# Lightning attention and a leaky-ReLU MLP on one core: k and q block loads on SyncE's queue, three chunks at a time

## The chip, the cores and the metric

The kernel runs on one core of one Trainium2 chip. Times are device microseconds of that core; the metric is the median over several runs of the whole kernel.

## What is computed

Inputs are `q`, `k`, `v` (4 batches, 8 heads, 768 positions, head size 64), a decay `lam` per head, and weights `w_in` (512 x 2048) and `w_out` (2048 x 512), which arrive as 64-bit floats and are turned into 32-bit ones on the chip. The reference, cut to what matters:

```
for b in range(nb):                       # blocks of 64 positions
    intra = einsum('bhic,bhjc->bhij', qb, kb) * Dmask      # lam ** (i - j), i >= j
    intra = einsum('bhij,bhjd->bhid', intra, vb)
    inter = einsum('bhid,bhde->bhie', qb * lam_pow, kv_state)
    out[:, :, sl] = intra + inter
    kv_state = lam_block * kv_state + einsum('bhsd,bhse->bhde', kb * rev_pow, vb)
x = out.transpose(0, 2, 1, 3).reshape(3072, 512)
h = x @ w_in
return maximum(0.01 * h, h) @ w_out
```

## The kernel before

The 3072 rows of x are 24 chunks of 128 tokens, six groups of four chunks. Every value in the MLP is split into three parts (h, l, m), so that each product is made of three products on TensorE.

Stages. First, attention of the first chunks and the conversion of `w_in` (to about 96 us in the profile). Then "rounds", one per chunk, mixed with "up" products, which are x times `w_in` for one group and one of eight slices of 256 columns of d_ff. Last, the "down" products with `w_out` (L658, from 354 us). An up product for a whole group (L599) has six blocks of four matmuls of 512 columns on the PSUM banks b10, b11 and b2; ACT rescales a bank (L617), then applies leaky ReLU into one of two `gs` buffers (L620), and SP stores `gs` to `G` in DRAM (L623). The down stage reads `G` back (L633).

A round (`round_of`, L487) has the own block's product into `po` (L291), then the next chunk's scores and state update into `psc` (L291), then the second half of the inter-block product into `po`. Before that second half, TensorE waits for `seen_po`, a copy of two columns of `po` by DVE or ACT (L448). Then ACT and DVE make xh, xl and xm of the chunk (L464, L465, L467). DVE multiplies the scores by the decay (L409), POOL scales k and q (L379, L383).

How k and q come in. The products need k and q with head dimension on partitions (`kTs`, `qTs`, two buffers each, by chunk parity). Up to chunk 11 TensorE transposes them (L363). From chunk 12 (`DV`) `load_subs` (L325) loads blocks of 32 x 32 elements so that a DVE transpose of 32 x 32 squares (`turn`, L340, its instruction L343) finishes the work: 16 loads of 32 KB for k and 16 for q, each for two chunks. k goes by SP's queue into `raw[2]`, q by ACT's queue, first into `raw[1]`, then into q's former buffer in `att`. k in its natural form and v are loaded as well (L316, L348), on SP.

`w_out` in the meantime: `w_out` (L573) loads each slice's two halves (512 KB each, L526, SP's queue) into `raw[0]` or `raw[1]`; ACT makes three pieces (L535, L537, L539), DVE joins them (L541, L542) into `w32`, and SP stores that to DRAM (L576). `w_out_parts` (L578) reads it back (L580) into buffers that lie over attention's `att` memory, once attention is over, and makes h, l and m of it (L548, L550, L553, L559), in the place of `w_in`'s parts.

What sets the order. A program-time planner (`Plan`, L37 on) records each operation with an engine, an estimated duration, its dependencies and a rank (the place in the list `seq`, L696, plus an offset), and `emit` (L81) lays them out engine by engine: at each step the operation that can start first, then the lowest rank. A result counts as there after the duration and a lag; for a DMA the lag is 3.5 us:

```
LAG = {"PE": 0.25, "ACT": 0.1, "DVE": 0.1, "POOL": 0.12, "DMA": 3.5}
ends[u].append((free[e], e))
```

"DMA" stands for SP's queue. Each engine and each queue then runs its list strictly in this order. `seen_po` may go to DVE or ACT, as the planner finds. In `seq`, the first 41 entries are written by hand (they reach round 11); then come 32 up products of the groups 2 to 5, with the rounds from 12 to 23 after every second one, and one `w_out` slice after every third.

Of the kernel before, what the change touches and what calls it, by code (L numbers as in the profile page):

```python
# [36 lines left out]
class Plan:  # L37
# [7 lines left out]
    def __init__(self):  # L45
        self.ops, self.last, self.rank = [], {}, 0.0
        self.chain, self.chains = None, {}
        self.warm = 0.0
        self.first = {"PE": 0.0, "ACT": 0.0, "DVE": 3.4, "POOL": 0.0, "DMA": 0.2}
        self.cold, self.idle, self.spare = 6.0, None, None  # L50
# [10 lines left out]
    def add(self, eng, us, fn, reads=(), writes=(), rank=0.0):  # L61

        n, deps = len(self.ops), set()
        for k in reads:
            w, r = self.last.setdefault(k, [None, []])
            if w is not None:
                deps.add(w)
            r.append(n)
        for k in writes:
            w, r = self.last.setdefault(k, [None, []])  # L70
            if w is not None:
                deps.add(w)
            deps.update(r)
            self.last[k] = [n, []]
        deps.discard(n)
        ways = {eng: us} if isinstance(eng, str) else dict(zip(eng, us))
        if self.chain is not None:
            self.chains[self.chain].append(n)
        self.ops.append((ways, fn, deps, (self.rank + rank, n), set(writes)))

    def emit(self):  # L81
# [30 lines left out]
        while len(done) < n:  # L112
# [23 lines left out]
            for u in users[i]:  # L136
                ends[u].append((free[e], e))
                left[u] -= 1
                if not left[u]:
                    for x in self.ops[u][0]:  # L140
                        able[x].add(u)
# [19 lines left out]
def kernel(  # L161
# [28 lines left out]
    NRAW = 3  # L190
    SUBQ, SUBR, SUBD = ("DMA", "ACT"), 5.0, 0.0

    DV = 12
    C4 = P // 4
    HALF = (slice(0, D), slice(D, 2 * D))
    assert DV % 2 == NCB % 2 == 0 and D == 64 and KO == HP == 4 and SEQ % C == 0 and NCH % GC == 0 and d_model == T == 512 and NP % 4 == 0

# [21 lines left out]
    lows = [sb([P, d_model], f"low{i}", I32) for i in range(2)]  # L219
    w32 = sb([P, 2, d_model], "w32")  # L220
    tt = [raw[-1][:, i * T:(i + 1) * T] for i in range(2)]
    gs = [sb([P, 2, T], f"gs{i}") for i in range(2)]
# [3 lines left out]

    NA = 8608
    att = sb([P, NA], "att")
# [8 lines left out]
    ident = part(P)  # L237
    kqv_f = [part(2 * H * D) for _ in range(3)]
    kqv = [[x[:, i * H * D:(i + 1) * H * D].rearrange("p (h d) -> p h d", h=H) for i in range(2)] for x in kqv_f]
# [23 lines left out]
    plan.idle, plan.spare, plan.warm = busy, "b10", 1.3 + 0.22 * WARM  # L263
    add = plan.add

    def factors_k():
# [42 lines left out]
    def load_kq(c):  # L309
        b, n, i = of(c)  # L310
        for src, x, nm in ((k, 0, "k"), (q, 1, "q")):
            y, dst = src[b, :, n * C:(n + 1) * C, :], kqv[x][i]

            def go(y=y, dst=dst):
                for z in range(2):
                    nc.sync.dma_start(out=dst[:, z * HP:(z + 1) * HP, :], in_=y[z::2].rearrange("h p d -> p h d"))  # L316
            if nm == "k" or c < DV:
                add("DMA", 1.15 if c < DV else 1.5, go, [], [f"{nm}{i}"])

    def subs(c):  # L320

        two = ((k, raw[-1], [f"raw{NRAW - 1}"]), (q, raw[-2], [f"raw{NRAW - 2}"]) if c < DV + 2 else (q, kqv_f[1], ["q0", "q1"]))
        return [(x, y.rearrange("p (y t) -> p y t", y=HP), keys) for x, y, keys in two]

    def load_subs(c):  # L325
        b, n, i = of(c)
        for nm, eng, (src, sub, keys) in zip("kq", SUBQ, subs(c)):
            add("DVE", 0.0, lambda: None, [], keys)
            for y in range(HP):
                for a in range(4):  # L330
                    h = y // 2 + (2 * y + a // 2) % HP * 2
                    z = src[b, h, n * C:(n + 2) * C, a % 2 * C4:(a % 2 + 1) * C4]
                    o = sub[a * C4:(a + 1) * C4, y, :]
                    add(eng, 0.58 if eng == "DMA" else 0.45,
                        lambda o=o, z=z, e=nc.sync if eng == "DMA" else nc.scalar: e.dma_start(  # L335
                            out=o.rearrange("j (m i) -> j m i", i=C4), in_=z.rearrange("(m j) i -> j m i", j=C4)),
                        keys, [f"{nm}s{y}{a}"], rank=SUBR + SUBD * (4 * y + a))
            add("DMA", 0.0, lambda: None, [f"{nm}s{y}{a}" for y in range(HP) for a in range(4)], [f"{nm}s"])

    def turn(c):  # L340
        i = c % 2
        for nm, (_, sub, keys), dst in zip("kq", subs(c - i), (kTs[i], qTs[i])):
            add("DVE", 0.7, lambda a=dst, b=sub: nc.vector.transpose(out=a, in_=b[:, :, i * C:(i + 1) * C]),  # L343
                keys + [f"{nm}s"] + [f"{nm}s{y}{a}" for y in range(HP) for a in range(4)], [f"{nm}T{i}"])

    def load_v(c):
        b, n, i = of(c)
        add("DMA", 1.15, lambda: nc.sync.dma_start(out=kqv[2][i], in_=v[b, :, n * C:(n + 1) * C, :].rearrange("h p d -> p h d")),  # L348
            [], [f"v{i}"])
# [137 lines left out]
    def round_of(c):  # L487
# [14 lines left out]
        if DV <= c + 3 < NCH:  # L502
            turn(c + 3)
        if DV <= c + 4 < NCH and c % 2 == 0:
            load_subs(c + 4)
# [7 lines left out]
    def to_float32(kind, p, h, dst, key, after=()):  # L513

        nonlocal n_raw
        j, n_raw = n_raw % (len(raw) - (kind == "wo")), n_raw + 1
        r, low, kl = raw[j], lows[n_raw % 2], f"low{n_raw % 2}"
        d = dst.bitcast(I32)

        def load():  # L520
            r64 = r.bitcast(I64)
# [11 lines left out]

        add("DMA", 1.6, load, after, [f"raw{j}"])
        add("ACT", 0.67, lambda: nc.scalar.activation(out=dst, in_=words(1, F32), func=AF.Abs, scale=2.0 ** -110),  # L535
# [25 lines left out]

    w32f = w32.rearrange("p h n -> p (h n)")

    def w_in(p):
# [7 lines left out]

    def w_out(p, after):  # L573
        for h in range(2):
            to_float32("wo", p, h, w32[:, h, :], f"w32{h}", after)
        add("DMA", 1.5, lambda: nc.sync.dma_start(out=WO[p], in_=w32f), ["w320", "w321"], [f"WO{p}"])  # L576

# [9 lines left out]
    def up(g, p, lo=0, hi=GC):  # L587
# [20 lines left out]
        for fs in blocks:  # L608
# [9 lines left out]
            for i, f in enumerate(fs):  # L618
                add("PE", us, lambda f=f, d=b[:, i, :]: product(d, f, 2), keys("m"), [kb])
            add("ACT", ns, lambda b=b, r=r: nc.scalar.activation(out=r, in_=b, func=AF.Prelu, bias=0.0, scale=1.0 / WS, alpha=0.01),  # L620
                [kb], [f"gs{jg}"], rank=-1.5)
        add("DMA", 1.5 * (hi - lo) / GC + 0.1,
            lambda: nc.sync.dma_start(out=G[g][p].rearrange("p (f t) -> p f t", f=2)[:, :, toks], in_=y), [f"gs{jg}"], [f"G{g}{p}"])  # L623

# [21 lines left out]
    def down(g, p):  # L646

        nonlocal n_t
        for tb in range(GC):
# [51 lines left out]
           ("up", 1, 4)]  # L701
    nxt, n_out = 3 * GC, 0
    steps = [(g, p) for g in range(2, NG) for p in range(NP)]
    for n, (g, p) in enumerate(steps):
# [4 lines left out]
        if nxt < NCH and nxt // GC < g + 2 and n % 2 == 0:  # L709
            seq.append(("r", nxt))  # L710
            nxt += 1
        if n_out < NP and n % 3 == 1:
            seq.append(("wo", n_out, ["G%d%d" % steps[n - 1]]))
            n_out += 1
# [7 lines left out]
    for n, x in enumerate(seq):  # L722
        plan.rank = float(n)
        if x[0] in "abr":
            {"a": alone, "b": begun, "r": round_of}[x[0]](x[1])
# [48 lines left out]
```

## Time and profile before

| | |
|---|---|
| runs | 621.29, 622.35, 626.31 us |
| median | 622.35 us |
| profiled execution's own time | 623.09 us |
| its span | 621.3 us |
| granted TensorE clock, mean | 0.996 |

Transfers that the change touches (from the profile's list of DMA issues; the last column is the median time from issue to landing):

| transfer | queue, line | count | size | us to landing |
|---|---|---|---|---|
| k blocks into `raw` | SP, L335 | 96 | 32 KB | 2.5 |
| q blocks into `att` | ACT, L335 | 80 | 32 KB | 3.0 |
| q blocks into `raw` | ACT, L335 | 16 | 32 KB | 2.6 |
| `w_out` halves | SP, L526 | 16 | 512 KB | 5.9 |
| stores of `gs` to `G` (whole groups) | SP, L623 | 45 | 512 KB | 3.4 |
| v | SP, L348 | 24 | 256 KB | 4.3 |

How to read the profile: PE is TensorE's matmuls and PEld its weight loads, DVE is VectorE, ACT ScalarE, POOL GpSimd; SPq and ACTq are DMA issues on the queues of SyncE and ScalarE. A timeline row has start, length, engine, line, operation, output<-input, size and count; in brackets the idle time just before it and what ended it. Busy TensorE time has modelled ends, so gaps are best read from start to start. The medians above are of one execution.

### The profile page before, as it was taken

Reading aid. Unit: us, or ns where it says so; the run is one execution under the profiler, and the core shown is the slowest. Engines: PE = TensorE matmul, PEld = TensorE weight load, DVE = VectorE, ACT = ScalarE, POOL = GpSimd, SP = SyncE. Lnnn points to the kernel's source line nnn. Section 1 sums busy time; section 2 is a strip of 40 time slices with the busy share of each in tenths; the row PEclk is TensorE's granted clock in tenths of the full one; section 3 lists DMA queues with packets and bytes.
Section 4 is the critical chain, followed back from the end, with each engine's and each line's share of the span. In section 5 each row is a group of like instructions: output and inputs, shape, how many; then the busy total and the mean of one; then the engine's idle time right before and its main releaser. Section 6 shows DMA issues by size and latency. Waiting matters only on the chain.

```text
span 621.3 us, 13134 instructions
## 1 busy us (share of the span) xinstructions
PE 606.5 (98%) x5482; PEld 504.4 (81%) x5482; DVE 306.9 (49%) x401; ACT 266.8 (43%) x426; POOL 90.9 (15%) x95
## 2 busy tenths in 40 slices
PE   8799999999999998999999999999999999999997
PEld 7588987898888877888778888888888888888885
DVE  4679883610354335434255863735545454535531
ACT  3598884334456455556564622312222312214111
POOL 4752422410223123221000000000000000000000
PEclk9899999999999999999999999999999999999999
DMA  9888867572788878885765752433424333433201
GB/s 202 222 254 266 230 190 165 137 160 104 207 203 233 248 202 231 208 252 187 258 232 212 245 192 69 164 108 101 170 71 142 127 111 126 135 103 120 84 1 68
DMA packets 143259, 104.68 MB, mean 168 GB/s; under 512 B 118112, under 2 KB 120160, under 8 KB 143200
## 3 DMA queue, kind: packets, MB, share of 16 engines
q1 hardware_dynamic: 112592, 92.30, 48.9%
q10 hardware_dynamic: 30608, 11.55, 7.6%
q8 instruction: 43, 0.70, 0.5%
q14 instruction: 16, 0.13, 0.1%
HBM read 68.16 MB, written 35.65 MB: 167 GB/s over the span
## 4 chain that ended last, share of the span: by engine, by line
PE 87%; DMA 8%; ACT 2%; DVE 1%; SPq 1%; issue 1%; POOL 0%; DVEq 0%; ACTq 0%
PE b L599 37%; PE b L658 18%; PE po L658 11%; PE psc L658 11%; DMA att<-in_q_dram 4%; PE pt L658 3%; PE po L291 3%; PE psc L291 3%; DMA att<-in_v_dram 2%; DMA att<-in_k_dram 1%; DMA raw<-in_moe_w_out_dram 1%; PE pt L363 1%; SPq L335 1%; ACT low L537 1%; PE b L258 1%
## 5 line engine op out<-in xcount | busy, mean ns | idle before, releaser
L640 ACT ACTIVATE xh<-att 128x1024 fp32r<-128x1024 f32 x48 | 50.9, 1061 | 147.3 <-PE po L658 145.9
L641 DVE SCALAR_TENSOR_TENSOR xl<-att,xh 128x1024 fp32r<-128x1024 f32 x48 | 58.7, 1223 | 99.4 <-ACT xh L640 99.3
L599 PE MATMUL b<-xh,wh 128*128 128x512 f32 (+3 forms) x416 | 105.8, 377 | 0.0
L599 PE MATMUL b<-xm,wm 128*128 128x512 f32 (+3 forms) x416 | 104.6, 382 | 0.8 <-ACT b L617 0.8
L599 PE MATMUL b<-xl,wl 128*128 128x512 f32 (+3 forms) x416 | 105.2, 376 | 0.0
L599 PEld LDWEIGHTS b<-xl,wl 128*128 128x128 f32 x416 | 75.5, 188 | 14.5
L599 PEld LDWEIGHTS b<-xh,wh 128*128 128x128 f32 x416 | 75.0, 188 | 14.2
L599 PEld LDWEIGHTS b<-xm,wm 128*128 128x128 f32 x416 | 73.3, 188 | 16.2 <-ACT b L617 2.3
L620 ACT ACTIVATE gs<-b 128x512 f32<-128x512 f32 (+2 forms) x98 | 57.7, 589 | 54.7 <-PE b L599 46.9
L617 ACT ACTIVATE b<-b 128x512 f32<-128x512 f32 (+2 forms) x98 | 55.8, 576 | 59.1 <-PE b L599 47.2
L658 PE MATMUL b<-wh,xh 128*128 128x512 f32 x192 | 74.7, 389 | 0.0
L658 PE MATMUL b<-wl,xl 128*128 128x512 f32 x192 | 74.7, 389 | 0.0
L643 DVE SCALAR_TENSOR_TENSOR xm<-xl,xh 128x1024 fp32r<-128x1024 f32 x48 | 58.8, 1226 | 4.8
L383 POOL TENSOR_TENSOR att<-att 128x512 f32<-128x512 f32 (+1 forms) x24 | 30.3, 1263 | 83.9 <-PE po L291 31.1
L658 PEld LDWEIGHTS b<-wh,xh 128*128 128x128 f32 x192 | 36.0, 187 | 7.6
L658 PEld LDWEIGHTS b<-wl,xl 128*128 128x128 f32 x192 | 36.1, 188 | 7.4
L419 POOL TENSOR_TENSOR att<-att 128x256 f32<-128x256 f32 x40 | 33.7, 843 | 38.5 <-DVE att L416 35.0
L409 DVE TENSOR_TENSOR att<-psc,att 128x512 f32<-128x512 f32 x24 | 16.5, 688 | 43.4 <-PE psc L291 43.4
L658 PE MATMUL po<-wm,xm 128*128 128x512 f32 (+1 forms) x100 | 37.2, 381 | 0.7 <-ACT raw L680 0.7
L658 PE MATMUL pt<-wm,xm 128*128 128x512 f32 x96 | 37.3, 389 | 0.0
L658 PE MATMUL b<-wm,xm 128*128 128x512 f32 x96 | 37.3, 389 | 0.0
L658 PE MATMUL psc<-wh,xh 128*128 128x512 f32 x96 | 37.3, 389 | 0.0
(69 smaller groups left out, 785.3 us busy)
## 6 DMA issues: line engine op xcount, KB each, us to landing
att<-g SPq DMA_DIRECT2D x48, 512.0 KB, 3.3
g<-gs SPq DMA_DIRECT2D x45, 512.0 KB, 3.4
raw<-in_moe_w_in_dram ACTq DMA_DIRECT2D x16, 512.0 KB, 5.0
raw<-in_moe_w_out_dram SPq DMA_DIRECT2D x16, 512.0 KB, 5.9
att<-in_k_dram SPq DMA_DIRECT2D x48, 128.0 KB, 4.0
att<-in_v_dram SPq DMA_DIRECT2D x24, 256.0 KB, 4.3
out_dram<-gs SPq DMA_DIRECT2D x23, 256.0 KB, 2.0
wo<-w SPq DMA_DIRECT2D x8, 512.0 KB, 3.2
```

Of the source, the lines that this page charges most:

```text
L258: nc.tensor.transpose(out=b1[0][:, 0:P], in_=ident, identity=ident)
L291: nc.tensor.matmul(dst[HALF[cols]], lhsT=lhsT[HALF[rows]], rhs=rhs[HALF[rows]], start=start, stop=True, skip_group_check=True)
L383: add(eng, us, lambda: e.tensor_tensor(o, x, _bc(pow_q, 2, 2)[:, :, m, :], op=ALU.mult), ["fq", dep], [f"qsT{i}"])
L409: add("DVE", 0.69, lambda: nc.vector.tensor_tensor(sc, psc[:, :, lower, :], decay, op=ALU.mult), ["psc", "fk"], ["sc"])
L419: add("POOL", 0.7, lambda new=new, j=j: nc.gpsimd.tensor_tensor(state[(j + 1) % 4], new, _bc(lam_c, 2, D), op=ALU.mult), [f"st{j % 4}", "f ...
L599: nc.tensor.matmul(dst, lhsT=w[z][:, kk * 2 * P + f * P:kk * 2 * P + (f + 1) * P], rhs=x[z][:, kk, toks], start=start and kk == 0, stop=kk ...
L617: add("ACT", ns, lambda b=b: nc.scalar.activation(out=b, in_=b, func=AF.Copy, bias=0.0, scale=S + 1.0), [], [kb], rank=-1.5)
L620: add("ACT", ns, lambda b=b, r=r: nc.scalar.activation(out=r, in_=b, func=AF.Prelu, bias=0.0, scale=1.0 / WS, alpha=0.01), [kb], [f"gs{jg} ...
L640: add("ACT", 1.05, lambda: nc.scalar.activation(out=h, in_=graw[j], func=AF.Copy, bias=0.0, scale=NEAR), reads, wr("h"))
L641: add("DVE", 1.25, lambda: nc.vector.scalar_tensor_tensor(l, graw[j], 1.0, h.bitcast(F32), op0=ALU.mult, op1=ALU.subtract), reads + [f"rh{ ...
L643: add("DVE", 1.25, lambda: nc.vector.scalar_tensor_tensor(m, l.bitcast(F32), -S, h.bitcast(F32), op0=ALU.mult, op1=ALU.add), [f"rh{j}", f" ...
L658: nc.tensor.matmul(acc[tb][z // 2][:, cols], lhsT=ring[j][z][:, f * T + tb * P:f * T + (tb + 1) * P], rhs=W[pp][z][:, f * d_model:(f + 1) ...
```

## The change

Block loads: both k and q go by SP's queue, 48 KB each, for three chunks instead of two. k lies in two pieces in `raw[1]` and `raw[2]`; q of chunks 12 to 14 in three pieces in `w32` and the two `lows`, later in q's former buffer, made longer by 512 elements per partition. One DVE transpose per piece. `w_out` keeps `raw[0]` alone, and its halves are entries of `seq` of their own, one after each up product until all 16 are placed.

Planner: loads and stores made by `move` in the later part (`steady`: rounds, up products and `w_out` entries after the hand-written list) count with 0.5 us of queue time (1.0 for k's pair, 0.75 for a block load) instead of a transfer's duration, with 4 us (2 us for stores of `gs`) added before a result counts as there, and with a rank offset of -8. Block loads have rank offsets of their own: from 4.0 up by 0.2 for each of the 16 places (earlier part) or 0.4 (later part). The first two blocks (chunks 12 to 17) are made in the earlier part, with 0.55 us each; the other two in the later part.

The core of the diff:

```diff
-        self.warm = 0.0
+        self.warm, self.slack, self.more = 0.0, 0.0, {}
...
+        if self.slack:
+            self.more[n] = self.slack
...
-                ends[u].append((free[e], e))
+                ends[u].append((free[e] + self.more.get(i, 0.0), e))
...
-    SUBQ, SUBR, SUBD = ("DMA", "ACT"), 5.0, 0.0
+    TURN = 3
+    SLACK, GSLACK = 4.0, 2.0
+    SUBL, FIRST = 0.75, -8.0
...
-    NA = 8608
+    NA = 9120
...
-    kqv_f = [part(2 * H * D) for _ in range(3)]
+    kqv_f = [part(2 * H * D + (TURN - 2) * HP * C * (i == 1)) for i in range(3)]
...
+    steady = False
+
+    def length(us, issue=0.5):
+
+        return issue if steady else us
+
+    def move(us, fn, reads, writes, issue=0.5, rank=0.0, slack=SLACK):
+
+        plan.slack = slack if steady else 0.0
+        if steady and not rank:
+            rank = FIRST
+        add("DMA", length(us, issue), fn, reads, writes, rank=rank)
+        plan.slack = 0.0
...
-                add("DMA", 1.15 if c < DV else 1.5, go, [], [f"{nm}{i}"])
+                move(1.15, go, [], [f"{nm}{i}"], issue=1.0)
 
     def subs(c):
 
-        two = ((k, raw[-1], [f"raw{NRAW - 1}"]), (q, raw[-2], [f"raw{NRAW - 2}"]) if c < DV + 2 else (q, kqv_f[1], ["q0", "q1"]))
-        return [(x, y.rearrange("p (y t) -> p y t", y=HP), keys) for x, y, keys in two]
+
+        n = TURN * C
+        def rows(x, lo, hi):
+            return x[:, :(hi - lo) * n].rearrange("p (y t) -> p y t", t=n), lo, hi
+        ks = [(*rows(raw[-2], 0, 2), [f"raw{NRAW - 2}"]), (*rows(raw[-1], 2, 4), [f"raw{NRAW - 1}"])]
+        if c < DV + TURN:
+            return ks, [(*rows(w32f, 0, 2), ["w320", "w321"])] + [
+                (*rows(lows[i].bitcast(F32), 2 + i, 3 + i), [f"low{i}"]) for i in range(2)]
+        return ks, [(*rows(kqv_f[1], 0, HP), ["q0", "q1"])]
 
     def load_subs(c):
         b, n, i = of(c)
-        for nm, eng, (src, sub, keys) in zip("kq", SUBQ, subs(c)):
-            add("DVE", 0.0, lambda: None, [], keys)
...
-                    add(eng, 0.58 if eng == "DMA" else 0.45,
-                        lambda o=o, z=z, e=nc.sync if eng == "DMA" else nc.scalar: e.dma_start(
-                            out=o.rearrange("j (m i) -> j m i", i=C4), in_=z.rearrange("(m j) i -> j m i", j=C4)),
-                        keys, [f"{nm}s{y}{a}"], rank=SUBR + SUBD * (4 * y + a))
...
+        for nm, src, pieces in zip("kq", (k, q), subs(c)):
+            for sub, lo, hi, keys in pieces:
+                add("DVE", 0.0, lambda: None, [], keys)
...
+                        move(0.55, lambda o=o, z=z: nc.sync.dma_start(
+                                out=o.rearrange("j (m i) -> j m i", i=C4), in_=z.rearrange("(m j) i -> j m i", j=C4)),
+                            keys, [f"{nm}s{y}{a}"], issue=SUBL, rank=4.0 + (0.4 if steady else 0.2) * (4 * y + a))
 
     def turn(c):
...
-            add("DVE", 0.7, lambda a=dst, b=sub: nc.vector.transpose(out=a, in_=b[:, :, i * C:(i + 1) * C]),
...
+            for sub, lo, hi, keys in pieces:
+                add("DVE", 0.1 + 0.15 * (hi - lo), lambda a=dst[:, lo:hi, :], b=sub: nc.vector.transpose(out=a, in_=b[:, :, m * C:(m + 1) * C]),
...
-        if DV <= c + 4 < NCH and c % 2 == 0:
+        if DV <= c + 4 < NCH and (c + 4) % TURN == 0:
             load_subs(c + 4)
...
-        j, n_raw = n_raw % (len(raw) - (kind == "wo")), n_raw + 1
+        j, n_raw = n_raw % (1 if kind == "wo" else len(raw)), n_raw + 1
...
-        add("DMA", 1.6, load, after, [f"raw{j}"])
+        move(1.6, get, after, [f"raw{j}"])
...
-    def w_out(p, after):
-        for h in range(2):
-            to_float32("wo", p, h, w32[:, h, :], f"w32{h}", after)
-        add("DMA", 1.5, lambda: nc.sync.dma_start(out=WO[p], in_=w32f), ["w320", "w321"], [f"WO{p}"])
+    def w_out(p, h, after):
+        to_float32("wo", p, h, w32[:, h, :], f"w32{h}", after)
+        if h == 1:
+            move(1.5, lambda: nc.sync.dma_start(out=WO[p], in_=w32f), ["w320", "w321"], [f"WO{p}"])
...
-        if n_out < NP and n % 3 == 1:
-            seq.append(("wo", n_out, ["G%d%d" % steps[n - 1]]))
+        if n_out < 2 * NP and n >= 1:
+            seq.append(("wo", n_out // 2, n_out % 2, ["G%d%d" % steps[n - 1]]))
             n_out += 1
...
+        steady = begin <= n and x[0] in ("r", "up", "wo")
```

The loads of v and the stores of `gs` to `G` go through `move` in the same way.

## The prediction

> **What bounds the kernel now.** I read first the page's busy table, then the windows view cut at the stages, then TensorE's gaps in the stage that the diff touches, and last what the other engines did before the longest gap.
>
> ```profile
> span 621.3 us, 13134 instructions
> PE 606.5 (98%) x5482; PEld 504.4 (81%) x5482; DVE 306.9 (49%) x401; ACT 266.8 (43%) x426; POOL 90.9 (15%) x95
> ```
>
> By stage (window, its length, then busy time of PE, PEld, DVE, ACT, POOL with instruction counts, granted clock, DMA share, GB/s):
>
> ```profile
> 0.00:96.00 96.00, 89.52 (x1532) 75.66 (x1533) 73.30 (x119) 67.00 (x118) 42.94 (x44) 0.98 0.85 224
> 96.00:320.00 224.00, 220.09 (x2641) 183.09 (x2640) 81.31 (x143) 116.92 (x207) 47.93 (x52) 1.00 0.72 202
> 320.00:608.00 288.00, 288.00 (x1271) 238.44 (x1272) 149.48 (x136) 80.47 (x99) 0.00 (x0) 1.00 0.38 128
> ```
>
> TensorE sets the end. Of 621.3 us it idles 14.8: 6.5 before 96 us, 3.9 between 96 and 320 us, nothing in the down projection, 4.4 in the tail. The new kernel's TensorE order holds the same 1567 rows, moved about from 96 us on; the first third and the tail are untouched. So this change can only work on the 3.9 us, or add to them. Gaps in this stage, from TensorE's timeline (the bracket is idle time and releaser):
>
> ```profile
> 99.36 1.07 PE L599 MATMUL b<-xl,wl 128*128 128x512 f32 x4
> 100.88 1.20 PE L599 MATMUL b<-xm,wm 128*128 128x512 f32 x4 [0.46 <-ACT b L617]
> ...
> 217.78 1.11 PE L291 MATMUL psc<-att 64*64 64x64 f32 x64
> 219.40 0.46 PE L291 MATMUL po<-att 64*64 64x64 f32 x16 [0.51 <-DVE att L448]
> ...
> 235.38 1.11 PE L291 MATMUL psc<-att 64*64 64x64 f32 x60
> 238.69 0.45 PE L291 MATMUL po<-att 64*64 64x64 f32 x8 [2.19 <-DVE att L448]
> ```
>
> Idle understates a stall, since ends are modelled; I count from start to start. Four products of 512 columns take 0.91; the first gap took 1.52, a loss of 0.61. From the 64 psc products to the next po ones an unstalled round takes 0.93 (250.94 to 251.87); here 1.62 and 3.31, losses of 0.69 and 2.38. By the same count the gaps at 260.75 (1.20 for 0.93), 299.72 (1.21 from po to po, where 0.72 is enough) and 319.84 (1.46 for 0.91) lose 0.27, 0.49 and 0.55. Together 5.0 us: all that there is to gain.
>
> What stands before the worst of them:
>
> ```profile
> 228.22 1.29 SPq L526 DMA_DIRECT2D raw<-in_moe_w_out_dram  x2
> ...
> 231.62 0.58 ACT L617 ACTIVATE b<-b 128x512 f32<-128x512 f32 x1 [1.74 <-DMA g<-gs]
> 234.30 0.32 ACTq L335 DMA_DIRECT2D att<-in_q_dram  x1
> 234.72 0.60 ACT L620 ACTIVATE gs<-b 128x512 f32<-128x512 f32 x1 [2.52 <-PE b L599]
> 236.49 0.37 ACTq L335 DMA_DIRECT2D att<-in_q_dram  x1
> 236.96 0.60 ACT L620 ACTIVATE gs<-b 128x512 f32<-128x512 f32 x1 [1.64 <-PE psc L291]
> 237.45 0.65 ACT L535 ACTIVATE w<-raw 128x512 f32<-128x512 f32 x1
> ...
> 238.14 0.43 DVE L541 TENSOR_SCALAR w<-w 128x512 int32<-128x512 int32 x1 [15.27 <-ACT w L535]
> 238.48 0.15 DVE L448 COPY att<-po 128x2 f32<-128x2 f32 x1
> ```
>
> Both queues take their completion semaphores from one set of eight in turn (the built order names them; their counts in the trace are 57 or 58 each). An issue on ACT therefore waits for the transfer that used its semaphore last, often SP's. The two 512 KB w_out loads issued at 228.22 and 228.72 land 6.1 and 7.3 us later; ACT's q loads at 234.30 and 236.49 go just when these land. Behind them ACT is late, DVE's L541 is late for ACT's L535, and the small copy L448, which lets the second half of the round go on, stands behind L541. Counted for line 335, ACT's own work waited 16.9 us for these q issues (L617 9.6, L620 4.6, L464 1.4, L535 1.3).
>
> **The change part by part.**
>
> *q's block loads leave ACT.* Before: 96 k loads on SP and 96 q loads on ACT, 32 KB each. After: 128 loads of 48 KB (four blocks of three chunks, 16 for each of k and q), all on SP. ACT is freed of 80 issues at 0.347 us and 16 at 0.418, 34 us of its 224, and of the 16.9 us above, which mostly overlap them. [...] By the rows, the wait that comes with an issue counts: it holds ACT for 2 to 3 us at a time. [...] I follow the rows: the gap at 100.88 is ACT's L617 directly behind q issues.
>
> *SP pays.* 32 more small issues at the median 0.45 us: 14 us. A burst costs more: eight k loads took 5.33 us at 100.30 and 5.49 at 256.24, 0.67 to 0.69 each. Densest stretch of the built order: 52 issues between six stores of g, which are six up products of 5.44 us (24 x 0.227) and two rounds of 2.1, 36.9 us of TensorE. At 0.45 SP needs 23, at 0.69 it needs 36. Next densest: 46 in 31.4 us, 32 at the burst price. So SP holds its pace between these ends, nearly saturated at the upper. I take 0.55, between, as w_out loads and rows of 12 instead of 8 pieces lie among them. Bytes are the same; packets of 128 bytes take 13 ns each, 24 per DMA engine and load, 0.31 us, below SP's issue.
>
> *Later loads rank behind all others, with slack in the plan.* The plan adds 4 us (2 for stores of g) to each planned landing. Before, a w_out load was planned to be in use 5.1 us (1.6 + 3.5) after its issue; the trace says 4.0/5.9/7.3 (min/median/max). After: 0.5 + 4 + 3.5 = 8.0. So ACT's L535 no longer meets a load in flight unless SP runs over 2.1 us late. That removes the second cause of the 2.38 gap. In the built order L448's copies stand 17 times on ACT, 7 on DVE (10 and 14 before), so fewer stand behind L541 and block transposes. The transposes themselves kept DVE waiting 5.6 us at 128.8 and 3.2 at 210.3; the later one is followed by the 0.69 gap. Value of this part: the 0.69 and what the first part leaves of the 2.38.
>
> *One staging buffer for w_out instead of two, halves one by one.* Each half is 5.9 landing and 2.1 of ACT, about 8 us; 16 of them 128 to 144 us, inside the 156 to 335 us that the order gives. Price on TensorE 0; uncovered, the next half is late and ACT waits at L535 with evictions queued behind.
>
> *Transposes in pieces.* 24 of 0.69 us become 42 (15 for chunks 12 to 14, 27 after). Bounds for the 18 extra: 0 to 18 x 0.15 (the smallest DVE copy here), 2.7 us of DVE, which is 36% busy in this stage; 0 on the path.
>
> *Rounds move.* Summed in products, rounds 18, 21, 22 and 23 come 12.7, 21.8, 13.6 and 10 us later; eight up products (43.5 us) still follow the last, and two blocks cover the xh, xl, xm of the last chunk. The att buffers come free 10 us later, so do the first w_out re-loads (298.7 to about 309); their first use waits for TensorE anyway. 0.
>
> Sum: of 5.0 us, 0.61 + 0.69 + 2.38 + 0.27 = 3.95 go; 0.49 stays (nothing follows the last round's copy), 0.55 stays in some place. New stalls on a fuller SP, bounds 0 and what rival two says; I take 0.95. Net -3.0: 623.1 for the profiled execution (span 621.3 to 618.3). The median shown is 622.35, 0.7 below that execution's own 623.09: **619.4**.
>
> **Rivals.**
>
> *It moves the waits and removes none.* SP is FIFO: behind a late block load stand stores of g, v and k. For it: SP itself waits up to 4.7 us at 231.46 to 236.15 behind the same landings. Against: planned slack, and SP's waits cost TensorE only through buffers. Time: 622.3 (621 to 624).
>
> *SP becomes the bound, slower.* Place: the three late blocks. A g store may be late by about 4 us (its buffer is wanted 7.5 us later, less 3.3 landing), and three PSUM banks hold some 1.8 more. If issues cost over 0.71 us in the dense stretch (36.9/52), or landings hold them (w_out, 7.3), SP is late by more than 6 us and TensorE pays what is over. At 0.85 the stretch needs 44, 7 late; with w_out waits of 2 to 3 on top, some 3 over, in three blocks 9: 619.4 + 9 = 628. Against: the plan reckons 0.75 for each such load.
>
> *All goes:* 622.35 - 5 = 617.4.
>
> **How the numbers follow.** Likeliest 0.58 (619.4, range 618 to 621), waits moved 0.22, SP bound 0.14, all gone 0.06. Over 1% (below 616.1) needs more than there is: 0.02. Over 628.6: half of SP bound, 0.08. Within 1%, what a measurement here can tell: 0.90. Range 617.0 to 625.5 leaves out most of SP bound and little below.
>
> **What would show it.** No ACTq rows in 96 to 320 us, TensorE idle there near 1.5 us, gaps at L448's heirs gone; SP's small issues at 0.45 to 0.69. Wrong if ACT waits for w_out landings, if evictions wait for stores of g, or if TensorE's idle rises above 5.

## The result and the profile after

The changed kernel takes 617.47 us (median of 8 runs, 616.78 to 620.23) against 624.19 us (8 runs, 621.29 to 626.51) for the kernel before: ratio 0.9903, 95% interval 0.9874 to 0.9931. Run again later it gave 616.91 us and 0.9902 (0.9878 to 0.9927). The prediction was 619.4 us, 3.0 us under its base of 622.35; the gain is 6 to 7 us. Direction and mechanism held, the size was half. That 619.4 comes within 2 us is in part luck: the median of three runs that it started from lies 1.8 us under the median of eight. One of e2's six executions took 1257 us, twice the others, and is left out below.

The page of the changed kernel, then its stages (window, length, busy time of PE, PEld, DVE, ACT, POOL with counts, granted clock, DMA share, GB/s):

```profile
span 615.4 us, 13097 instructions
PE 604.8 (98%) x5482; PEld 503.8 (82%) x5482; DVE 306.9 (50%) x409; ACT 270.7 (44%) x436; POOL 90.6 (15%) x95
```

```profile
0.00:96.00 96.00, 90.06 (x1537) 76.46 (x1538) 77.04 (x119) 68.22 (x120) 44.41 (x45) 1.00 0.88 229
96.00:320.00 224.00, 223.69 (x2663) 187.05 (x2662) 81.17 (x152) 118.53 (x214) 46.19 (x51) 1.00 0.72 202
320.00:604.00 284.00, 283.99 (x1253) 234.61 (x1252) 146.59 (x134) 82.20 (x101) 0.00 (x0) 1.00 0.38 128
```

TensorE now idles 0.3 us between 96 and 320 us, where it idled 3.9. (L599 is now L623, L617 L641, L620 L644, L448 L474, L343 L369, L335's block loads L361, L535 L561, L526 L552, L623 L647.) The one gap left in TensorE's timeline of that stage that is worth a line is the one after the last round, with nothing to fill it:

```profile
298.26 0.93 PE L310 MATMUL po<-att 64*64 64x64 f32 x48
299.48 0.46 PE L310 MATMUL po<-att 64*64 64x64 f32 x16 [0.28 <-DVE att L474]
```

What the worst stall had before it, now in ACT's timeline (a round at 236 to 240 us): no issue stands among the ACT rows, the w_out pieces run without a wait for their load, and ACT is free and waits 0.28 us for TensorE's po before the small copy, where DVE's copy had stood behind L541.

```profile
234.83 0.76 ACT L565 ACTIVATE low<-raw 128x512 f16<-128x512 f32 x1
235.46 0.57 ACT L644 ACTIVATE gs<-b 128x512 f32<-128x512 f32 x1
235.93 0.65 ACT L561 ACTIVATE w<-raw 128x512 f32<-128x512 f32 x1
236.47 0.59 ACT L644 ACTIVATE gs<-b 128x512 f32<-128x512 f32 x1
237.32 0.58 ACT L641 ACTIVATE b<-b 128x512 f32<-128x512 f32 x1 [0.25 <-PE b L623]
238.18 0.16 ACT L474 COPY att<-po 128x2 f32<-128x2 f32 x1 [0.28 <-PE po L310]
```

SP's side: block loads at a median of 0.468 us an issue, with the transfers that others wait for let in between them (a late block in SP's timeline). Single issues take longer, 1.97 us at 210.05, 1.74 at 217.15 and 2.76 at 240.14. That is no wait for a completion semaphore (the transfers that had used theirs had landed 4.4, 2.1 and 3.8 us earlier), and the trace names no other cause; no stall of TensorE stands behind them.

```profile
213.15 0.41 SPq L647 DMA_DIRECT2D g<-gs  x1
213.60 0.43 SPq L361 DMA_DIRECT2D raw<-in_k_dram  x1
214.08 0.89 SPq L361 DMA_DIRECT2D att<-in_q_dram  x1
...
217.15 1.74 SPq L361 DMA_DIRECT2D raw<-in_k_dram  x1
218.99 0.41 SPq L552 DMA_DIRECT2D raw<-in_moe_w_out_dram  x1
219.44 0.43 SPq L361 DMA_DIRECT2D att<-in_q_dram  x1
219.97 0.41 SPq L647 DMA_DIRECT2D g<-gs  x1
```

Below, "stalls" are TensorE's losses counted from start to start: each matmul's step less the median step of its kind, where that is over 0.12 us. For 90 to 345 us the kernel before has 5.1 us by this count, the changed kernel 0.7. "Half clock" is the time between 90 us and the end of the down products for which the trace shows a granted TensorE clock of 0.5, be TensorE busy or waiting. Steps that such a clock makes longer count as stalls too: about 6 of e1's 22.3 us, and 1.5 to 3 us in e2, e4, e5, e6 and e8.

### The profile page after: what moved, and what is told of

Read it like the earlier page. It is cut to its first block, busy times and chain, and to the rows that moved or that the text cites. A ratio compares the mean times of both kernels' runs of the same rounds, so it can differ in the third digit from the quotient of the medians.

```text
span 615.4 us, 13097 instructions
## 1 busy us (share of the span) xinstructions
PE 604.8 (98%) x5482; PEld 503.8 (82%) x5482; DVE 306.9 (50%) x409; ACT 270.7 (44%) x436; POOL 90.6 (15%) x95
## 4 chain that ended last, share of the span: by engine, by line
PE 96%; DMA 2%; POOL 0%; SPq 0%; DVE 0%; issue 0%; ACT 0%; DVEq 0%
PE b L623 44%; PE b L682 18%; PE po L682 11%; PE psc L682 11%; PE po L310 4%; PE pt L682 4%; PE psc L310 4%; DMA att<-in_q_dram 2%; PE pt L389 1%; PE po L389 1%; PE b L263 1%; DMA att<-in_k_dram 1%; PE b L389 0%; SPq L335 0%; POOL att L405 0%
## 5 line engine op out<-in xcount | busy, mean ns | idle before, releaser
L664 ACT ACTIVATE xh<-att 128x1024 fp32r<-128x1024 f32 x48 | 50.9, 1061 | 145.9 <-PE po L682 144.0
L623 PE MATMUL b<-xh,wh 128*128 128x512 f32 (+3 forms) x416 | 105.8, 377 | 0.0
L623 PE MATMUL b<-xl,wl 128*128 128x512 f32 (+3 forms) x416 | 105.5, 377 | 0.0
L623 PE MATMUL b<-xm,wm 128*128 128x512 f32 (+3 forms) x416 | 104.8, 381 | 0.0
L623 PEld LDWEIGHTS b<-xl,wl 128*128 128x128 f32 x416 | 75.3, 188 | 14.5 <-DVE wl L579 0.2
L623 PEld LDWEIGHTS b<-xh,wh 128*128 128x128 f32 x416 | 75.0, 188 | 14.8 <-ACT gs L644 0.7
L623 PEld LDWEIGHTS b<-xm,wm 128*128 128x128 f32 x416 | 73.6, 188 | 14.5 <-ACT b L641 0.4
L641 ACT ACTIVATE b<-b 128x512 f32<-128x512 f32 (+2 forms) x98 | 56.3, 576 | 56.2 <-PE b L623 55.8
L644 ACT ACTIVATE gs<-b 128x512 f32<-128x512 f32 (+2 forms) x98 | 57.2, 587 | 43.5 <-PE b L623 39.9
L682 PE MATMUL b<-wh,xh 128*128 128x512 f32 x192 | 74.7, 389 | 0.0
L682 PE MATMUL b<-wl,xl 128*128 128x512 f32 x192 | 74.7, 389 | 0.0
L409 POOL TENSOR_TENSOR att<-att 128x512 f32<-128x512 f32 (+1 forms) x24 | 29.0, 1209 | 95.9 <-PE po L310 66.8
L682 PEld LDWEIGHTS b<-wl,xl 128*128 128x128 f32 x192 | 36.1, 188 | 7.6
L682 PEld LDWEIGHTS b<-wh,xh 128*128 128x128 f32 x192 | 36.0, 187 | 7.5
L405 POOL TENSOR_TENSOR att<-att 128x512 f32<-128x512 f32 (+1 forms) x24 | 28.4, 1182 | 73.0 <-PE po L389 34.2
L682 PE MATMUL po<-wm,xm 128*128 128x512 f32 (+1 forms) x100 | 37.2, 381 | 0.7 <-ACT raw L704 0.7
L682 PE MATMUL psc<-wh,xh 128*128 128x512 f32 x96 | 37.4, 389 | 0.0
L682 PE MATMUL psc<-wl,xl 128*128 128x512 f32 x96 | 37.3, 389 | 0.0
```

The costliest lines, as they stand in the source:

```text
L405: lambda e="POOL": ENG[e].tensor_tensor(kr[nr], kr[nr], _bc(pow_k, 3, D)[nr], op=ALU.mult), ["fk"], [f"k{i}"])
L409: add(eng, us, lambda: e.tensor_tensor(o, x, _bc(pow_q, 2, 2)[:, :, m, :], op=ALU.mult), ["fq", dep], [f"qsT{i}"])
L623: nc.tensor.matmul(dst, lhsT=w[z][:, kk * 2 * P + f * P:kk * 2 * P + (f + 1) * P], rhs=x[z][:, kk, toks], start=start and kk == 0, stop=kk ...
L641: add("ACT", ns, lambda b=b: nc.scalar.activation(out=b, in_=b, func=AF.Copy, bias=0.0, scale=S + 1.0), [], [kb], rank=-1.5)
L664: add("ACT", 1.05, lambda: nc.scalar.activation(out=h, in_=graw[j], func=AF.Copy, bias=0.0, scale=NEAR), reads, wr("h"))
L682: nc.tensor.matmul(acc[tb][z // 2][:, cols], lhsT=ring[j][z][:, f * T + tb * P:f * T + (tb + 1) * P], rhs=W[pp][z][:, f * d_model:(f + 1) ...
```

## The experiments

My theory (A) was that q's issues on ACT make ACT late, and that is most of the loss. Rivals: the planned landings are most of it (B); a fuller SP queue costs more than it brings (C). Each run is timed against the kernel before on the same chip.

| run | median us | ratio (95%) | stalls, 90 to 345 us | half clock, us |
|---|---|---|---|---|
| changed | 617.5 | 0.990 (0.987 to 0.993) | 0.7 | 0 |
| e1 q on SP alone | 638.9 | 1.025 (1.021 to 1.029) | 22.3 | 17.1 |
| e2 slack and rank alone | 629.3 | 1.010 (1.006 to 1.013) | 11.9 | 3.4 |
| e3 changed, q on ACT | 621.5 | 0.997 (0.995 to 0.999) | 5.0 | 0 |
| e4 changed, no slack | 627.9 | 1.008 (1.005 to 1.010) | 8.7 | 3.4 |
| e5 changed, two chunks | 625.4 | 1.005 (1.003 to 1.007) | 9.0 | 6.8 |
| e6 changed, no ranking | 630.5 | 1.013 (1.010 to 1.016) | 14.1 | 13.7 |
| e7 changed, no slack on g | 618.0 | 0.993 (0.991 to 0.996) | 2.0 | 0 |
| e8 before, again | 623.7 | 1.000 (0.998 to 1.003) | 7.8 | 3.4 |
| e9 changed, again | 616.9 | 0.990 (0.988 to 0.993) | 0.5 | 0 |
| e10 changed, early q on ACT | 623.0 | 1.000 (0.997 to 1.003) | 0.5 | 0 |
| e11 changed, slack 6 and 3 | 639.6 | 1.027 (1.024 to 1.030) | 1.3 | 20.5, all after 345 us |

**e1: q's block loads on SP, nothing else.**

```diff
-    SUBQ, SUBR, SUBD = ("DMA", "ACT"), 5.0, 0.0
+    SUBQ, SUBR, SUBD = ("DMA", "DMA"), 5.0, 0.0
```

> The kernel before with one edit: q's block loads go by SP's queue instead of ACT's (still two chunks a block, no slack in the plan). Theory A (ACT held by q issues is most of the loss): TensorE's stalls between 96 and 330 us, counted start to start, fall from 5.1 us to about 2, ratio to the kernel before about 0.995. Theory B (the planned landings are most of it): with loads of w_out still planned 5.1 us after their issue, ACT's L535 and the copy L448 go on meeting late loads; stalls stay at 4 to 6 us, ratio 0.998 to 1.002. Theory C (SP's queue too full without slack): stalls over 7 us, ratio over 1.004.

Measured: 15 us slower. Theory C, far beyond its bound. Its timeline (SP, ACT and TensorE in one) at the largest stall:

```profile
217.64 3.67 SPq L348 DMA_DIRECT2D att<-in_v_dram  x1
...
221.40 3.36 SPq L623 DMA_DIRECT2D g<-gs  x1
222.36 0.66 ACT L535 ACTIVATE w<-raw 128x512 f32<-128x512 f32 x1 [4.25 <-DMA raw<-in_moe_w_out_dram]
...
225.98 0.57 ACT L620 ACTIVATE gs<-b 128x512 f32<-128x512 f32 x1
...
226.60 2.08 PE L599 MATMUL b<-xh,wh 128*128 128x512 f32 x4 [4.59 <-ACT gs L620]
```

ACT met a w_out load in flight and stood 4.25 us; L620 came behind the pieces of two such loads, and TensorE, out of free banks, waited 4.59 us for it. In the whole run ACT's L620 waited 14.7 us in all for stores of g, which is rival two of the prediction. And then the last row: four products take 1.87 us to their neighbour's start instead of 0.91. The windows view of the same run shows why (after the length: PE, PEld, DVE, ACT, POOL, then the granted clock):

```profile
221.00:224.00 3.00, 1.00 (x5) 0.50 (x3) 0.95 (x2) 1.64 (x3) 0.00 (x0) 1.00 0.91 231
224.00:227.00 3.00, 0.40 (x1) 0.40 (x2) 2.78 (x5) 3.00 (x7) 1.79 (x2) 0.80 0.63 193
227.00:230.00 3.00, 3.00 (x8) 2.10 (x7) 0.50 (x1) 0.51 (x2) 0.84 (x1) 0.50 1.09 290
230.00:233.00 3.00, 3.00 (x113) 2.69 (x116) 0.00 (x0) 0.76 (x2) 0.22 (x1) 0.56 0.85 289
```

This stall is paid twice: 4.59 us of wait, and then a slow clock (0.50 from 227 to 230). The stretch at half clock is 6.8 us long; it begins at 225.8, 0.8 us before TensorE goes on, so TensorE runs 6.1 us in it and loses 3.0.

**e2: the planner's part alone** (the kernel before, with the slack, the issue times and the rank of -8 for all transfers but block loads; q stays on ACT, two chunks; w_out still comes in pairs of halves into two buffers, and the block loads keep one rank).

```diff
-                ends[u].append((free[e], e))
+                ends[u].append((free[e] + self.more.get(i, 0.0), e))
...
-        add("DMA", 1.6, load, after, [f"raw{j}"])
+        move(1.6, load, after, [f"raw{j}"])
```

> The kernel before with only the planner's part of the change: in the later part, transfers count with 0.5 us of queue, 4 us more (2 for stores of gs) before they count as there, rank -8; q's block loads stay on ACT's queue, two chunks a block. Theory A: ACT is still held by its q issues, stalls stay at 3 to 5 us, ratio 0.997 to 1.001. Theory B: the stalls behind late w_out loads go, 1 to 2 us are left, ratio about 0.994.

Measured: 6 us slower. Neither theory had this. ACT's work waited 27 us behind q issues (L632 11.8, L629 7.3 and 3.7, L476 4.1), where the kernel before had 16.9. In the waits view these 27 us end with landings of q's own earlier loads, which had used the semaphore, and 6 us more of ACT's waits with those of SP's transfers. Why that came to more than in the kernel before stays open.

**e3: the changed kernel with q back on ACT** (with slack on the landing of all of q's loads, as for the others).

```diff
-                        move(0.55, lambda o=o, z=z: nc.sync.dma_start(
...
+                        if nm == "k":
+                            move(0.55, fn, keys, [f"{nm}s{y}{a}"], issue=SUBL, rank=rank)
+                        else:
+                            add("ACT", 0.45, fn, keys, [f"{nm}s{y}{a}"], rank=rank)
```

> The changed kernel with q's block loads back on ACT's queue (three chunks a block and the slack kept). Theory A: ACT is held again, stalls 2 to 4 us, 2 to 3 us slower than the changed kernel, ratio to the kernel before about 0.994. Theory B: stalls stay under 1.5 us, ratio about 0.991, as the changed kernel.

Measured: ratio 0.997 against 0.990, some 4 us slower than the changed kernel, stalls 5.0 (1.86 and 1.65 the largest). Theory A, somewhat more than it asked. ACT's work again waited for landings behind its issues, 7.9 us for q's loads. With slack and ranks in place, q on ACT costs 4 us, the plan's new order included. Between e2 and e3 lie 8 us, for what e2 leaves out: three chunks a block, w_out's halves one by one, the block loads' own ranks. No run isolates w_out's part.

**e4: the changed kernel without slack.**

```diff
-    SLACK, GSLACK = 4.0, 2.0
+    SLACK, GSLACK = 0.0, 0.0
```

> The changed kernel with SLACK and GSLACK at 0; q stays on SP, three chunks a block, issue times of the plan kept. Theory A: the slack matters little, stalls 1 to 2 us, ratio to the kernel before 0.991 to 0.993. Theory B: loads are met in flight again, stalls 3 to 6 us, ratio 0.996 to 1.000.

Measured: 1.8% above the changed kernel. Theory B, and more. Its waits view (engine, line, awaited: us, times, longest) names the load:

```profile
ACT w L561 <- DMA raw<-in_moe_w_out_dram: 13.0, 7, 3.9
ACT low L563 <- DMA raw<-in_moe_w_out_dram: 6.3, 7, 1.7
```

Without slack a w_out load is planned to be in use 4.0 us (0.5 + 3.5) after its issue. In the changed kernel the first of these waits is 0.6 us, once, and the second is not there. The parts that A and B name are both needed: with q on SP, the slack is worth 10 us, and with the slack, q's move is worth 4.

**e5: two chunks a block.**

```diff
-    TURN = 3
+    TURN = 2
```

> The changed kernel with blocks of two chunks instead of three: 192 loads of 32 KB on SP's queue, slack and ranks kept. If the number of issues on SP is what matters (a fuller SP delays stores of gs): 64 more issues at 0.45 to 0.69 us, TensorE's stalls between 90 and 345 us rise from 0.7 to 4 us or more, ratio to the kernel before 0.997 to 1.010. If slack and ranks alone carry the gain: stalls under 1.5 us, ratio about 0.991.

Measured: 1.5% above the changed kernel. The largest stall is one wait of TensorE for DVE's transposes (L369), 3.7 us; 0.5 us before its end begin 6.8 us at half clock. The block loads that they read were issued up to 252.86 and landed at 255.64, 0.8 us after TensorE had begun to wait; then DVE still had L567 and L568 before them, late for ACT's L561, up to 257.1. So three chunks are part of the gain, with the same bytes. That the 64 issues do it, and not the plan's other order, fits this trace but isn't shown apart.

**e6: no ranking.**

```diff
-    SUBL, FIRST = 0.75, -8.0
+    SUBL, FIRST = 0.75, 0.0
...
-                            keys, [f"{nm}s{y}{a}"], issue=SUBL, rank=4.0 + (0.4 if steady else 0.2) * (4 * y + a))
+                            keys, [f"{nm}s{y}{a}"], issue=SUBL, rank=5.0)
```

> The changed kernel without the ranking: rank offset of the other transfers 0 instead of -8, block loads 5.0 all alike instead of 4 to 10. Slack, issue times and three chunks kept. If the order on SP's queue matters beyond the slack: stores of gs stand behind block loads again, stalls 3 to 8 us, ratio 0.997 to 1.005. If slack and count are enough: stalls under 1.5 us, ratio about 0.991.

Measured: 2.3% above the changed kernel. One stall makes most of it. SP's and TensorE's rows of its timeline:

```profile
247.14 7.50 SPq L361 DMA_DIRECT2D att<-in_q_dram  x12
...
252.87 0.93 PE L310 MATMUL po<-att 64*64 64x64 f32 x48
...
254.74 1.12 SPq L552 DMA_DIRECT2D raw<-in_moe_w_out_dram  x1
255.91 0.94 SPq L361 DMA_DIRECT2D att<-in_q_dram  x2
256.95 0.42 SPq L374 DMA_DIRECT2D att<-in_v_dram  x1
...
261.17 1.13 PE L310 MATMUL psc<-att 64*64 64x64 f32 x32 [7.37 <-DMA att<-in_v_dram]
```

One load of v stands behind 14 block loads and a w_out load. TensorE waits 7.4 us for it. The clock is halved for 13.7 us, from 256.4 on, of which TensorE spends 4.8 in this wait and 8.9 at work, 4.5 us lost. Slack did not help; my reading is that it counts from the planned issue and that the issue itself was late (the planned time is not on record).

**e7: no slack on stores of g.**

```diff
-    SLACK, GSLACK = 4.0, 2.0
+    SLACK, GSLACK = 4.0, 0.0
```

> The changed kernel with the slack of 2 us taken from the stores of gs alone; the 4 us of the other transfers kept. If without slack it is the stores of gs that TensorE is held by: most of what the run without any slack lost comes back, stalls 3 to 6 us, ratio 0.998 to 1.004. If it is the loads (w_out, blocks, k, v): stalls under 1.5 us, ratio about 0.991.

Measured: stalls 2.0, ratio 0.993 with an interval that overlaps the changed kernel's: between the two expectations on stalls, nearer the second. The stall that it has more, 1.5 us, has no store of g in its past: ACT stood 2.74 us at L561 for a w_out load in flight, L644 was late behind it, and TensorE waited for L644. (The load is issued at 218.97, in the changed kernel at 218.99; there ACT runs three evictions more before its L561 and waits 0.6 us.) So what the slack does is done in the main by the loads' 4 us.

**e8: the kernel before, a second profile.** No edit.

> The kernel before unchanged, for a second profile. Its first third is the same code as the changed kernel's. If the 1.4 us by which the two profiles differ beyond the stalls after 96 us is scatter of the start: the first 90 us again differ by up to 1.5 us from either. If the kernel before pays in some executions for a stall with a lower TensorE clock behind it: the granted clock falls below 0.9 in some stretch after 96 us, and that execution is 2 us or more longer.

Measured: the same time, but this execution (span 623.8 us) lost 7.8 us where the first lost 5.1. Its stall at L448 is again there, and this time TensorE's rows after it slow down (1.71 us from start to start for four products); the windows view has the clock of that stretch:

```profile
236.61 1.11 PE L291 MATMUL psc<-att 64*64 64x64 f32 x60
239.63 0.45 PE L291 MATMUL po<-att 64*64 64x64 f32 x8 [1.91 <-DVE att L448]
240.00 1.40 PE L599 MATMUL b<-xh,wh 128*128 128x512 f32 x4
241.20 1.91 PE L599 MATMUL b<-xl,wl 128*128 128x512 f32 x4
242.91 1.71 PE L599 MATMUL b<-xh,wh 128*128 128x512 f32 x4
```

```profile
236.00:246.00 10.00, 8.10 (x131) 6.68 (x129) 6.40 (x12) 6.83 (x12) 3.08 (x3) 0.83 0.76 192
246.00:256.00 10.00, 10.00 (x163) 8.29 (x163) 3.35 (x8) 4.33 (x8) 3.30 (x4) 1.00 0.76 243
```

3.4 us at half clock, 1.7 us lost, behind a stall of 2.1 us. In the first profile a stall of 2.4 us had no such tail. So the kernel before paid for it in one of two profiles.

What tells the two apart, by my reading, is where the stall lies. In each trace all changes of the clock lie on one grid of steps of 3413 ns (in the first profile of before one step at half clock, from 22.155 to 25.568 us, then 174 steps, 593.919 us, at full clock). These are the steps around the stall, two of the first profile of before, then one of this run (length, busy time of PE, PEld, DVE, ACT, POOL, clock):

```profile
233.77:237.18 3.41, 2.72 (x109) 2.15 (x107) 0.00 (x0) 0.82 (x2) 0.00 (x0) 1.00 0.61 128
237.18:240.60 3.42, 1.91 (x15) 1.58 (x16) 2.18 (x5) 3.42 (x7) 0.20 (x1) 1.00 0.53 153
237.42:240.83 3.41, 1.50 (x30) 1.16 (x21) 1.41 (x4) 2.93 (x6) 0.00 (x0) 1.00 0.41 114
```

The first profile's stall is split, 0.7 and 1.5 us of idle time; this run's lies in one step, 1.9 us, and the clock halves at that step's end, 240.8. Over all profiles, from 90 us to the end of the down products and by the trace's modelled ends, the clock fell at the end of every full-clock step with 1.9 us idle or more (nine, 1.91 to 3.41) and of none with 1.7 or less; of two with 1.83 it fell after one (e4) and not after the other (e2, in its stall of 3.2 us).

**e9: the changed kernel, a second profile.** No edit.

> The changed kernel once more, for a second profile and as the neighbour of the next two. If its gain is that no stall near 2 us is left after 90 us: stalls between 90 and 345 us under 1 us again, no stretch at half clock after 90 us, ratio to the kernel before 0.988 to 0.993.

Measured: as expected. The stage's only stall is the 0.49 us after the last round.

**e10: q's loads of chunks 4 and 5 on ACT's queue**, the one attempt at a faster version that TensorE's early waits suggested.

```diff
+            act = nm == "q" and c in (4, 5)
...
-                    nc.sync.dma_start(out=dst[:, z * HP:(z + 1) * HP, :], in_=y[z::2].rearrange("h p d -> p h d"))
+                    e.dma_start(out=dst[:, z * HP:(z + 1) * HP, :], in_=y[z::2].rearrange("h p d -> p h d"))
```

> The changed kernel with q's loads of chunks 4 and 5 in the first 30 us on ACT's queue, where TensorE still waits up to 1.3 us for q on SP's queue. If SP's order is what makes these late: the waits of the first 90 us (3.7 us start to start) fall by about 1.5 us, 1 to 1.5 us faster than the changed kernel. If the eight shared semaphores and the transfers themselves are: no change within 0.2%.

Measured: 1% slower than the changed kernel. Losses of the first 90 us went from 4.8 in its neighbour to 8.4: TensorE now waits 2.1 us, in two waits, for copies on ACT; before one of them ACT had stood 1.7 us behind a q issue. The later rounds' gain stays. Neither expectation; ACT looks like the wrong place for these issues early on, too. But this profile also has 3.4 us at half clock from 17.9 us on, which its neighbour has not, and the planner's order of that stage differs throughout, so this run doesn't separate the causes.

**e11: more slack.**

```diff
-    SLACK, GSLACK = 4.0, 2.0
+    SLACK, GSLACK = 6.0, 3.0
```

> The changed kernel with slack 6 and 3 instead of 4 and 2. If slack only needs to cover the spread of landings, nothing is left to gain: stalls 0.5 to 1.5 us, as the changed kernel within 0.2%. If more slack pushes loads or rounds so late that products lack work: stalls 3 us or more, ratio to the kernel before over 0.995.

Measured: the stage itself keeps stalls of 1.3 us, yet the run is 3.7% above the changed kernel. The price lies after it: 22 us of stalls beyond 345 us, slow steps in 20.5 us at half clock included. Its waits view for TensorE:

```profile
PE b L682 <- ACT xh L664: 12.9, 2, 9.5
PE pt L389 <- DMA att<-in_q_dram: 2.8, 3, 1.9
PE b L682 <- DVE xl L665: 1.4, 2, 0.9
```

L682 and L664 are the down products and their xh. In SP's order a w_out load and the store after it stand among the first loads of the down stage; with 2 us more for each of 16 halves they are issued at 351.6 and 365.6, where the changed kernel has them at 322.8 and 334.4, and the down stage starts late. The shorter wait of TensorE, 3.4 us at 365.1, ended with an L664 that stood behind a half's pieces on ACT, the longer, 9.5 us at 384.0, with one that had waited 7.7 us for a load of `G`. That these loads are late for standing behind w_out's on SP is my reading. Slack is taken from the next stage's start.

## Why the prediction was right, and where its size was off

*All that there is to gain: 5.0 us.* Right for the stalls of the profiled execution: 5.1 became 0.7, and 0.5 in the second profile. Not right for the kernel's time, which fell by 6 to 7 us: the working has no term for the clock (below).

*What goes: 0.61 + 0.69 + 2.38 + 0.27.* All four went. The 0.49 after the last round stayed, as said. The 0.55 that was to stay "in some place" went as well.

*New stalls, "I take 0.95".* Measured 0.19 and 0. This term and the last were the mis-sized ones in the sum: net -4.4 to -4.6 instead of -3.0. I had taken SP at 0.55 us an issue; it ran at 0.468. w_out's landings, whose halves no longer go in pairs, became shorter (4.7 us median, 6.1 at most, where 5.9 and 7.3 were taken). Others became longer, the stores of `w32` 5.8 us where 3.2 was measured and the re-loads 6.1 for 4.7, at no cost that TensorE shows.

*The step that was missing: what a stall does to the clock.* Nothing in the working asked what comes after a stall. After 90 us, stalls of 2.0 to 2.3 us were followed by 3.4 us at half clock in e2, e4 and the second profile of before, but 2.4 us in the first profile and 3.2 us in e2 were not. In e2, e4 and that second profile the clock fell 1.2 to 1.4 us after TensorE had gone on. With the stalls of 2.2 to 7.6 us in e1, e5 and e6 it fell while TensorE still waited, and TensorE then ran 3 to 8.9 us at half clock, half of that lost. Stalls up to 1.9 us (e3, e7) had no such stretch behind them. The lengths of the stretches (3.4, 6.8, 13.7 us) are all multiples of 3413 ns, and a step with 1.9 us idle sufficed (e8), so that, by my reading, whether a stall of 2 to 3.2 us was paid twice hung on where in the grid it fell. By the page, a stall like the 2.38 us of before could not cost more than itself; by the rows its like cost 1.7 us more in one of two profiles.

*The whole account.* Round 9's scores start at 93.5 us in the first profile of before and at 92.2 in the changed kernel's, in code that both share; in the second pair at 93.1 and 92.3. First pair: 621.3 to 615.4 is 5.9 us, of which 4.4 are stalls and 1.3 lie before round 9. Second pair: 623.8 to 614.7 is 9.1, of which 7.3 are stalls with their tail and 0.9 lie before round 9; 0.9 this count doesn't find. Medians differ by 6.0 to 6.7, between the pairs. The start is the clock's doing, too, and not the changed code's: both profiles of before, e2, e5 and e11 have one stretch of 3.4 us at half clock between 15 and 33 us, and their round 9 comes at 92.6 to 93.5; both profiles of the changed kernel, e1, e3, e4, e6 and e7 have none there, and it comes at 91.3 to 92.3. Each group has runs of either start. (e10 rearranges the start.)

The mean clock of each execution separates the two terms. One stretch of 3.4 us alone brings it to 0.997, so executions at 0.999 or 1.000 have none. Among these, before takes 621.6 us (median of 18 out of all 63) and the changed kernel 617.0 (6 of 12): 4.6 us, about what the stalls gave. The rest of the gain, 1.5 to 2 us, is in good part the clock: 45 of the 63 executions of before lie lower, and 6 of the 12; over all of them the means are 0.9963 and 0.9980, and that difference on 620 us is 1.1 us. How much of it is the stalls' tail and how much the chance of the start, the means don't tell.

*q's block loads leave ACT.* I took this part as worth up to 3.3: the two gaps in whose engines' past a wait for a q issue stands, 0.61 and 2.38, and 0.27. e3 says 4 us. One reading of the prediction's rows was half right: by the semaphores in the trace, the q load at 234.30 went when the w_out load of 228.22 landed (234.28), but the one at 236.49 had waited for ACT's own q load of 229.29, which landed at 236.47. All of the 16.9 us ended with landings of q's own loads; in the second profile, 8.6 us with q's and 8.6 with SP's. And the gain holds only inside this change. By itself the same edit costs 15 us (e1), which my 3.3 does not have.

*SP pays.* The rival "SP becomes the bound" is in the main the account of e6, and part of that of e1 and e5. Its place was right (stores of g, loads of v and k behind block loads), its trigger was not: it isn't the mean issue time over 0.71 us alone that decides, but which transfer stands behind the block loads in the queue (e6, with the changed kernel's issue count, takes 14 us more than it), and its price lacked the clock.

*Slack.* I gave it the 0.69 and a rest of the 2.38. With q on SP it carries 10 us (e4), since it keeps ACT from meeting w_out loads in flight. That the built order put L448's heir on ACT 17 times agrees with the trace, but no run isolates it.

*One staging buffer, transposes in pieces, moved rounds: 0.* TensorE has no gap that names them, and ACT waited for a w_out load once, 0.6 us. No run takes one of the three back, so what each is worth by itself is not shown.

## What to carry to other kernels

Here, taking issues off a compute engine paid once the queue that received them was ordered by who is waited for (without that 2.3% above the changed kernel, e6), and once the program's order assumed landings as late as the trace showed them (without that 1.8%, e4). The move alone (e1, 1.025) and the planner's part alone (e2, 1.010) each made this kernel slower. Look in the trace for the first transfer behind a burst in a queue (in e6 a load of v behind 14 block loads and a w_out load, for which TensorE waited 7.4 us), and ask who waits for it. Look behind a TensorE stall for the clock: here stalls of 2.0 us (e4) and 2.1 us (e8) had 3.4 us at half clock behind them, and those of 2.4 (before, first profile) and 3.2 us (e2) had none.

## What the runs showed of the hardware

- The stretches at half clock lasted multiples of 3413 ns on a fixed grid: 3.4 us in the first profile of before (from 22.16 us), in e2, e4 and e8, 6.8 in e5 and in the one of e1 from 225.8, 13.7 in e6. From 90 us to the end of the down products, over all profiles, the clock fell at the end of all nine full-clock steps with 1.91 to 3.41 us of TensorE idle, of one of the two with 1.83, and of none with 1.7 or less; earlier, in the first profile of before, it fell after a step with 1.68 (at 22.16) and not after one with 1.73 (at 28.98). The shortest stall that was followed by one took 2.0 us (e4); the 7.6 us of e6 were followed by 8.9 us of work at half clock, 4.5 us lost.
- In the first profile of before, 454 issues follow another one on their completion semaphore. None of them starts sooner than 0.016 us after that one's transfer has landed; 60 start within 0.1 us after it, 19 of these after a transfer of the other queue. ACT's q load at 234.30 went 0.02 us after a w_out load of SP's had landed, 6.1 us after that one's issue. In e2, ACT's work waited 27 us behind its q issues, for landings of q's own loads.
- SP's 349 DMA issues stand in the first profile of before in the order of the built program, and so do ACT's 113.
- Block loads of 48 KB in packets of 128 bytes took as long as those of 32 KB on SP's queue: 0.47 and 0.45 us to issue, 2.5 us from issue to landing (medians); such a packet took 13 ns in both (median of 49152 in each trace).
